# Transposing q on VectorE in 32x32 blocks, in a linear-attention and feed-forward kernel

## The chip, the cores and the metric

One core of a Trainium2 chip runs the whole program. The metric is device microseconds of one execution. The engines are TensorE (PE, with its weight loads as PEld), VectorE (DVE), ScalarE (ACT), GpSimd (POOL) and SyncE (SP), which issues all the DMAs here.

## The reference

Linear attention over 8 batches, 8 heads, 576 tokens and 64 places of d, then a feed-forward block over all 4608 tokens:

```python
q_s = softmax(q, over d)            # exp(q - max), divided by (sum + 1e-9)
k_s = softmax(k, over the tokens)
kv  = einsum('bhsd,bhse->bhde', k_s, v)
x   = einsum('bhsd,bhde->bhse', q_s, kv)     # then (tokens, 512)
h   = x @ w_in                                # 512 -> 2048
g   = h where h >= 1; 0 where h <= -1; (h + 1)**2 / 4 between
out = g @ w_out                               # 2048 -> 512
```

## The kernel before

Tokens are handled in 9 chunks of 512. For each chunk there are 16 units of feed-forward, one for each 128 columns of the 2048. A unit written 3.5 below is unit 5 of chunk 3. A unit's first half (`s1`, L679) is 12 matmuls of 128x512 into a PSUM tile `h`; then ACT does relu and square (`g_relu`, `g_square`), DVE the minimum (`g_min`, L698), ACT the high half (`g_hi`, `gh`), DVE the low half (`g_lo`, `gl`, L706); its second half (`s2`, L717) is 12 matmuls into four PSUM tiles `o`, which are copied to SBUF (`osb`) and stored at the end of a chunk. Each fp32 product is done as three fp32r matmuls of high and low parts. PE does s1 of the next unit before s2 of this one, so the chain of relu to g_lo runs beside PE's work. `h` has two buffers, `r` (the relu's output) three.

While chunk c is in the feed-forward, the attention of chunk c+1 is prepared in four parts, one for each pair of heads (0 to 3). A tile name such as `q_4_1` is chunk 4, pair 1. For a pair:

- k: loaded, maximum over the tokens (`k_max`, tile `m2`, DVE; then `partition_all_reduce` on POOL), subtracted on DVE (`k_sub`), exponential on ACT, and multiplied with v on PE (`kv_mm`, 20 small matmuls into `kv`). Its reciprocal sums (`kv_z`), high part (`kv_hi`, ACT) and low part (`kv_lo`, DVE) follow. Chunks 0 and 1 handle k in another way, and chunk 8 has no k.
- q: loaded as 128 token rows by 4 x 128, maximum over each 64 places on DVE (`q_max`), subtracted on POOL (`q_rows`), exponential on ACT (`q_exp`), summed on DVE (`q_sum`, with the added constant and the reciprocal), multiplied on POOL (`q_rows`), transposed on PE with four 128x128 matmuls against an identity (`q_tr`, tile `tp` in PSUM), then split into a high part (`q_hi`, ACT) and a low part (`q_lo`, DVE).
- `x_mm` on PE multiplies the two with kv; `x_hi` and `x_lo` split the result for s1 of the next chunk.

The order of instructions on every engine is written out by a planner (`Plan`): each operation is given an engine, an estimated time, a due time and what it depends on, and buffers are represented by rings. The planner's list is then emitted as it is, so each engine works through its queue in order, and an instruction that waits holds up all that stands behind it on its engine. The small tiles of the pool `sm` (maxima and sums) have no ring in the plan; the tile framework adds the waits that their buffers need. `port=True` tells the planner to keep an operation apart from others on the port that DVE and POOL share. In chunks from 2 on, `q_tr` and `kv_mm` are one operation of the plan.

Of the kernel before, what the change touches and what calls it, by code (L numbers as in the profile page):

```python
# [11 lines left out]
F32 = mybir.dt.float32  # L12
# [16 lines left out]
NF = DF // P  # L29


NLOAD, NST, NR = 2, 4, 3

KT = 2

WARM = 9

# [39 lines left out]
class Plan:  # L77
# [103 lines left out]
def tile_linear_attention_then_ffn(  # L181
# [18 lines left out]
    nc = tc.nc  # L200
    NB = k.shape[0] + KT
    NT = out.shape[0]
# [8 lines left out]
    wk = ctx.enter_context(tc.tile_pool(name="wk", bufs=1))  # L211
# [3 lines left out]
    sm = ctx.enter_context(tc.tile_pool(name="sm", bufs=4))  # L215
# [23 lines left out]
    def ring(tag, n):  # L239
        return rings.setdefault(tag, Ring(n))  # L240
# [86 lines left out]
    xs, xdone, kvdone, kvread, kfs = {}, {}, {}, {}, []  # L327

    def attention(c, pr, due, step, slack):


        n = f"{c}_{pr}"
        first = c == 0
        after = 0.0 if first else START
        has_k = c < NB
        t = {}

        def at(stage):
# [46 lines left out]
        rpk, rpq = room(f"ps {ktag}", 1), room(f"ps {qtag}", 1)  # L385
# [51 lines left out]
        def kv_mm():  # L437
            t["kv"] = kpool.tile([P, D + 1], F32, tag=ktag, name=f"kv_{n}")
            for j in range(KJ):
                r = slice(0, SR if c < KT and j == KJ - 1 else P)  # L440
                for i in range(2):
                    d = slice(i * D, (i + 1) * D)
                    nc.tensor.matmul(  # L443
                        t["kv"][d, :],
                        t["k"][r, j, d],
                        t["v"][r, j, i * (D + 1) : (i + 1) * (D + 1)],
                        start=(j == 0),
                        stop=(j == KJ - 1),
                        tile_position=(0, i * D),
                    )  # L450
# [30 lines left out]
        def kv_lo():  # L481
# [4 lines left out]
            for i in range(2):  # L486
# [7 lines left out]
                    ALU.subtract,  # L494
                )

        def q_max():
            t["qf"] = t["q"].rearrange("p j (h d) -> p (j h) d", h=2)
            t["qm"] = sm.tile([P, 2 * NJ], F32, tag="qm", name=f"qm_{n}")
            nc.vector.tensor_reduce(t["qm"], t["qf"], AX.X, ALU.max)  # L500

        def q_rows(what, alu):
            def emit():
                rows = t[what].unsqueeze(2).broadcast_to([P, 2 * NJ, D])
                nc.gpsimd.tensor_tensor(t["qf"], t["qf"], rows, alu)  # L505

            return emit

# [1 line left out]
            nc.scalar.activation(t["q"], t["q"], AF.Exp)  # L510

        def q_sum():
            z = sm.tile([P, 2 * NJ], F32, tag="qz", name=f"qz_{n}")
            nc.vector.tensor_reduce(z, t["qf"], AX.X, ALU.add)
            nc.vector.tensor_scalar(z, z, EPS, None, ALU.add)
            t["qrz"] = sm.tile([P, 2 * NJ], F32, tag="qrz", name=f"qrz_{n}")
            nc.vector.reciprocal(t["qrz"], z)  # L517

        def q_tr():
            t["tp"] = qpool.tile([P, NJ, P], F32, tag=qtag, name=f"tp_{n}")  # L520
            for j in range(NJ):
                nc.tensor.transpose(t["tp"][:, j, :], t["q"][:, j, :], ident)  # L522
# [43 lines left out]
        kvready = []  # L566
        if has_k:
            if c < KT:
                et = room("ps h", 2) if first else rpq
                km = do("DVE", 0.75, 0, kt_max, lk)  # L570
                ke = do("ACT", 0.9, 1, kt_exp, km)
                kz = do("DVE", 0.32, 4, kv_z, ke)
                tr = do("PE", 0.75, 2, kt_tr, ke, *rpk.wait(), *et.wait())
# [5 lines left out]
                kc = do("ACT", 0.58, 2.5, kt_copy, tr, *rk.wait(), other=copies[0])  # L579
# [22 lines left out]
        if first or not has_k:  # L602
            tr = do("PE", 0.6, 3.6, q_tr, qn, *rpq.wait())
        else:

            def q_tr_kv_mm():
                q_tr()
                kv_mm()

            deps = [qn, ke, lv, *rpq.wait()] + ([kc] if c < KT else rpk.wait())  # L610
            tr = mm = do("PE", 1.3, 3.6, q_tr_kv_mm, *deps)
            if c >= KT:
                rpk.take(mm)
                kz = do("DVE", 0.32, 4, kv_z, mm)
            rk.free(mm)
        rpq.take(tr)
        rq.free(tr)
        if has_k:
            rv.free(mm)
            if first:  # L620
# [3 lines left out]
                kvready = [kf]  # L624
# [8 lines left out]
            else:  # L633
# [3 lines left out]
                kvready = [kl]  # L637
                rpk.free(kl)
        if first:
            qh = do(  # L640
                "ACT", 0.59, 4.1, q_32, tr, *rqh.wait(), other=[("DVE", 0.69, False)]
            )
            rqh.take(qh)
            xm = do("PE", 1.05, 4.5, x_mm32, qh, *kvready)
            early_users.append(xm)
            rqh.free(xm)
        else:
            rql = room("wk ql", 1)
# [4 lines left out]
            xm = do("PE", 0.8, 4.6, x_mm, ql, *kvready, kvdone.get((c - 1, pr)))  # L653
            rqh.free(xm)
            rql.free(xm)
            kvread[c - 1, pr] = xm
# [126 lines left out]
    for pr in range(NPAIR):  # L783
        attention(0, pr, 2.0 * pr, 1.5, 0.0)
# [90 lines left out]
```

## Time and profile before

| | |
|---|---|
| median of three runs | 891.9 us (891.73 to 892.34) |
| the profiled execution | 894.39 us, span 892.6 us |
| PE busy | 878.3 us, 98% |
| DVE busy | 429.2 us, 48% |
| ACT busy | 416.9 us, 47% |
| POOL busy | 140.1 us, 16% |

PE is the busy engine. Matmuls are pipelined, so the duration in a PE row is longer than the distance to the next start; what a matmul takes of PE's time is read from the starts. POOL's busy time leaves out what it spends between its own instructions around `partition_all_reduce`, where its idle time is put down to "issue".

### The profile page before, as it was taken

How to read it: one execution, taken by the hardware profiler on the slowest of the kernel's cores; microseconds unless marked ns; L12 is line 12 of the kernel's file. 1: busy time of each engine (PE TensorE's matmuls, PEld its weight loads, DVE VectorE, ACT ScalarE, POOL GpSimd, SP SyncE). 2: the span in 40 equal slices, each digit the busy share in tenths (PEclk: the TensorE clock that was granted, in tenths of full speed). 3: DMA queues.
4: the chain of work that ended last, by engine and by line, in shares of the span. 5: the costliest groups of instructions: out<-in, count | busy, mean ns of one | idle time of the engine just before them, and what ended most of it. 6: DMA issues, size and time to landing. Idle time of an engine off the chain costs nothing.

```text
span 892.6 us, 11623 instructions
## 1 busy us (share of the span) xinstructions
PE 878.3 (98%) x4486; PEld 722.8 (81%) x4486; DVE 429.2 (48%) x817; ACT 416.9 (47%) x736; POOL 140.1 (16%) x136
## 2 busy tenths in 40 slices
PE   7899999999999999999999999999999999999997
PEld 6588887888888888888888888888888888888886
DVE  6989865444544444454444444445434333323221
ACT  6787754443444444344434544444443444433333
POOL 5554521111111101111011110111011000000000
PEclk8999999999999999999999999999999999999999
DMA  8466512111211120020111121112100000000001
GB/s 320 163 218 208 194 68 78 42 42 42 89 42 42 42 81 27 28 79 24 66 42 42 43 89 42 42 42 89 42 14 12 36 24 12 1 17 32 1 1 47
DMA packets 24247, 57.27 MB, mean 64 GB/s; under 512 B 2688, under 2 KB 2688, under 8 KB 24192
## 3 DMA queue, kind: packets, MB, share of 16 engines
q1 hardware_dynamic: 24192, 56.54, 19.0%
q8 instruction: 35, 0.57, 0.3%
q14 instruction: 20, 0.16, 0.1%
HBM read 47.09 MB, written 9.44 MB: 63 GB/s over the span
## 4 chain that ended last, share of the span: by engine, by line
PE 95%; DVE 2%; DMA 1%; issue 1%; ACT 1%; POOL 0%; SPq 0%; DVEq 0%; ACTq 0%; POOLq 0%
PE o L717 44%; PE h L679 43%; PE x L546 3%; PE kv L443 3%; PE tp L522 2%; DMA q<-in_q 1%; DVE st L291 0%; PE x L538 0%; DVE st L288 0%; PE ep L414 0%; DMA k<-in_kt 0%; POOL q L505 0%; DMA out<-osb 0%; DVE qm L500 0%; ACT osb L225 0%
## 5 line engine op out<-in xcount | busy, mean ns | idle before, releaser
L692 ACT ACTIVATE r<-h,half 128x512 f32<-128x512 f32 x144 | 99.2, 689 | 356.6 <-PE h L679 356.5
L698 DVE SCALAR_TENSOR_TENSOR h<-h,r 128x512 f32<-128x512 f32 x144 | 100.6, 699 | 313.9 <-ACT r L695 313.6
L717 PE MATMUL o<-wl,gh 128*128 128x512 f32 x576 | 228.6, 397 | 1.8 <-ACT gh L702 1.1
L679 PE MATMUL h<-xl,wh 128*128 128x512 f32 x576 | 226.2, 393 | 0.4 <-DVE xl L561 0.4
L717 PE MATMUL o<-wh,gl 128*128 128x512 f32 x576 | 225.5, 391 | 0.9 <-DVE gl L706 0.9
L679 PE MATMUL h<-xh,wl 128*128 128x512 f32 x576 | 224.6, 390 | 0.9 <-POOL wl L302 0.9
L717 PE MATMUL o<-wh,gh 128*128 128x512 f32 x576 | 224.9, 390 | 0.0
L679 PE MATMUL h<-xh,wh 128*128 128x512 f32 x576 | 224.3, 389 | 0.0
L706 DVE TENSOR_TENSOR gl<-h,gh 128x512 fp32r<-128x512 f32 x144 | 99.0, 687 | 73.4 <-ACT gh L702 73.1
L717 PEld LDWEIGHTS o<-wl,gh 128*128 128x128 f32 x576 | 108.4, 188 | 25.5 <-ACT gh L702 2.0
L717 PEld LDWEIGHTS o<-wh,gl 128*128 128x128 f32 x576 | 108.4, 188 | 25.3 <-DVE gl L706 2.2
L679 PEld LDWEIGHTS h<-xh,wl 128*128 128x128 f32 x576 | 108.1, 188 | 24.3 <-POOL wl L302 1.8
L679 PEld LDWEIGHTS h<-xl,wh 128*128 128x128 f32 x576 | 108.3, 188 | 23.5 <-DVE xl L561 0.8
L679 PEld LDWEIGHTS h<-xh,wh 128*128 128x128 f32 x576 | 108.3, 188 | 22.1 <-issue 0.2
L717 PEld LDWEIGHTS o<-wh,gh 128*128 128x128 f32 x576 | 108.5, 188 | 21.2
L702 ACT CAST gh<-h 128x512 fp32r<-128x512 f32 x144 | 84.2, 585 | 74.4 <-DVE h L698 74.1
L695 ACT ACTIVATE r<-r 128x512 f32<-128x512 f32 x144 | 91.1, 633 | 4.3
L505 POOL TENSOR_TENSOR q<-q,qm 128x512 f32<-128x512 f32 x36 | 39.2, 1091 | 224.1 <-issue 107.9
L505 POOL TENSOR_TENSOR q<-q,qrz 128x512 f32<-128x512 f32 x36 | 38.0, 1055 | 158.6 <-DVE qrz L517 111.9
L302 POOL TENSOR_TENSOR wl<-st,wh 128x512 fp32r<-128x512 f32 x32 | 43.0, 1360 | 46.4 <-ACT wh L298 45.1
L426 POOL PARTITION_ALL_REDUCE m<-m x24 | 17.4, 725 | 178.9 <-DVE m L393 118.9
L291 DVE SCALAR_TENSOR_TENSOR st<-st 128x512 uint32<-128x512 uint32 x32 | 29.3, 917 | 2.6 <-ACT st L285 0.2
(72 smaller groups left out, 595.1 us busy)
## 6 DMA issues: line engine op xcount, KB each, us to landing
st<-in_w SPq DMA_DIRECT2D x32, 512.0 KB, 4.5
v<-in_v SPq DMA_DIRECT2D x32, 325.0 KB, 4.3
q<-in_q SPq DMA_DIRECT2D x36, 256.0 KB, 3.4
out<-osb SPq DMA_DIRECT2D x36, 256.0 KB, 2.0
k<-in_k SPq DMA_DIRECT2D x24, 320.0 KB, 3.2
kt<-in_kt SPq DMA_DIRECT2D x4, 288.0 KB, 4.9
k<-in_kt SPq DMA_DIRECT2D x4, 288.0 KB, 3.2
```

The lines of the kernel that those rows point to most:

```text
L291: nc.vector.scalar_tensor_tensor(t["lw"], t["hw"], 3, t["lw"], ALU.logical_shift_left, ALU.bitwise_or)
L302: nc.gpsimd.tensor_tensor(lo, t["lw"].bitcast(F32), f32(hi), ALU.subtract)
L443: nc.tensor.matmul(t["kv"][d, :], t["k"][r, j, d], t["v"][r, j, i * (D + 1) : (i + 1) * (D + 1)], start=(j == 0), stop=(j == KJ - 1), tile ...
L505: nc.gpsimd.tensor_tensor(t["qf"], t["qf"], rows, alu)
L546: nc.tensor.matmul(t["x"][:, :, p0:p1], lhs, rhs[:, :, p0:p1], start=(i == 0), stop=(i == 2),)
L679: nc.tensor.matmul(t["h"], lhs[:, r], rhs, start=(cc == 0 and i == 0), stop=(cc == NPAIR - 1 and i == 2),)
L692: nc.scalar.activation(t["r"], t["h"], AF.Relu, bias=half[:, :1], scale=0.5)
L695: nc.scalar.activation(t["r"], t["r"], AF.Square)
L698: nc.vector.scalar_tensor_tensor(t["h"], t["h"], 1.0, t["r"], ALU.max, ALU.min)
L702: nc.scalar.copy(t["gh"], t["h"])
L706: nc.vector.tensor_tensor(t["gl"], t["h"], f32(t["gh"]), ALU.subtract)
L717: nc.tensor.matmul(outs[c, j], lhs[:, s], rhs, start=(f == 0 and i == 0), stop=(f == NF - 1 and i == 2),)
```

## The change

In chunks 2 to 8, q is laid out in memory so that a partition holds one of 32 tokens with one of four blocks of 32 places of d (two heads times two halves of d), and along the row lie 16 blocks of 32 places, each of another group of tokens. VectorE's transpose of 32x32 blocks then gives the tile that four transposes on PE gave, in SBUF instead of PSUM. A token's 64 places now lie in two quadrants of 32 partitions. So `q_max` and `q_sum` reduce over 32 places each, and `q_both` joins the two halves: four copies of 32x16 swap neighbouring quadrants, and one 128x16 operation takes the maximum or the sum of the two. The joined maximum (`qm`) has one buffer, the joined sum (`qrz`) two; before, they had four. `r` gets two buffers instead of three. `kv_mm` is an operation of its own on PE, without q. The buffer of `x` in PSUM is taken at `x_mm` instead of at the transpose. Chunks 0 and 1 stay as they were.

```diff
-NLOAD, NST, NR = 2, 4, 3
+NLOAD, NST, NR = 2, 4, 2
...
+QT, QB = 2, 32
+NQ = P // QB
...
+        rows = c < QT
+        nrow = 2 * NJ if rows else T // QB
+
+        def q_both(part, alu, tag):
+            if rows:
+                return part
+            other = sm.tile([P, nrow], F32, tag="qo", name=f"{tag}o_{n}", bufs=1)
+            both = sm.tile(
+                [P, nrow], F32, tag=tag, name=f"{tag}_{n}", bufs=1 + (tag == "qrz")
+            )
+            for i in range(NQ):
+                r, o = (slice(x * QB, (x + 1) * QB) for x in (i, i ^ 1))
+                nc.vector.tensor_copy(other[r], part[o])
+            nc.vector.tensor_tensor(both, part, other, alu)
+            return both
+
         def q_max():
...
-            nc.vector.tensor_reduce(t["qm"], t["qf"], AX.X, ALU.max)
+            qm = sm.tile([P, nrow], F32, tag="qz", name=f"qm_{n}", bufs=2)
+            nc.vector.tensor_reduce(qm, t["qf"], AX.X, ALU.max)
+            t["qm"] = q_both(qm, ALU.max, "qm")
...
             nc.vector.tensor_reduce(z, t["qf"], AX.X, ALU.add)
+            z = q_both(z, ALU.add, "qrz")
             nc.vector.tensor_scalar(z, z, EPS, None, ALU.add)
...
+        def q_blocks():
+            t["tp"] = wk.tile([P, NJ, P], F32, tag="qt", name=f"tp_{n}")
+            nc.vector.transpose(
+                t["tp"].rearrange("p j d -> p (j d)"), t["q"].rearrange("p j d -> p (j d)")
+            )
...
-        qm = do("DVE", 0.68, 0.5, q_max, lq)
+        qm = do("DVE", 0.68 if rows else 1.4, 0.5, q_max, lq)
...
-        qz = do("DVE", 1.13, 2.2, q_sum, qe)
+        qz = do("DVE", 1.13 if rows else 1.85, 2.2, q_sum, qe)
...
-            tr = mm = do("PE", 1.3, 3.6, q_tr_kv_mm, *deps)
...
+            rqt = room("wk qt", 1)
+            tr = do("DVE", 0.65, 3.6, q_blocks, qn, *rqt.wait(), port=True)
+            rqt.take(tr)
+            if has_k:
+                mm = do("PE", 0.95, 3.6, kv_mm, ke, lv, *rpk.wait())
...
-            ql = do("DVE", 0.69, 4.2, q_lo, qh, *rql.wait())
+            ql = do("DVE", 0.69, 4.2, q_lo, qh, *rql.wait(), port=not rows)
...
+    qb = qq[QT:].reshape(-1, NQ, QB, NJ, NPAIR, 2, D // QB, QB)
+    qb = qb.transpose(0, 4, 5, 6, 2, 3, 1, 7).reshape(-1, NPAIR, P, 2 * NJ * D)
```

The planner sets a new order from it. Three places show what moves. In the rows below, a line number, an operation, out<-in and a shape stand in a row, "x3" is a count, and the brackets name the engines and DMA queues that the instruction waits for.

PE, at unit 3.5, before: behind the last matmuls of s1 come the transposes of `q_4_1` and the kv product of the same pair, then s2 of unit 3.4.

```order
L679 MATMUL h_3_5_3301<-xl_3_3_2996,wh5_0_111 128x512
L679 MATMUL h_3_5_3301<-xh_3_3_2985,wh5_0_111 128x512
L679 MATMUL h_3_5_3301<-xh_3_3_2985,wl5_0_112 128x512
L522 MATMUL tp_4_1_3322<-ident_90,q_4_1_2904 128x128 [waits DMAHW4_49,PE_49,Pool_49]
L522 MATMUL tp_4_1_3322<-ident_90,q_4_1_2904 128x128 x3
L443 MATMUL kv_4_1_3327<-v_4_1_2910,k_4_1_2900 64x65 [waits DMAHW5_49,DMAHW3_49]
L443 MATMUL kv_4_1_3327<-v_4_1_2910,k_4_1_2900 64x65 x9
L717 MATMUL o_3_0_3143<-wl4_1_110,gh_3_4_3299 128x512 [waits Activation_49]
```

The same place on PE in the changed kernel:

```order
L728 MATMUL h_3_5_3457<-xl_3_3_3144,wh5_0_111 128x512
L728 MATMUL h_3_5_3457<-xh_3_3_3129,wh5_0_111 128x512
L728 MATMUL h_3_5_3457<-xh_3_3_3129,wl5_0_112 128x512
L447 MATMUL kv_4_1_3484<-v_4_1_3044,k_4_1_3042 64x65 [waits DMAHW6_49,DMAHW5_49,PE_49]
L447 MATMUL kv_4_1_3484<-v_4_1_3044,k_4_1_3042 64x65 x9
L766 MATMUL o_3_0_3298<-wl4_1_110,gh_3_4_3461 128x512 [waits Activation_49]
```

The kv product stands where it stood, without the transposes and without the wait for POOL.

DVE, at the start of chunk 1, before: from g_lo of unit 0.15 to g_lo of unit 1.0.

```order
L706 TENSOR_TENSOR gl_0_15_1468<-h_0_15_1415,gh_0_15_1462 128x512 [waits Activation_49]
L227 COPY osb_0_1_1495<-o_0_1_513 128x512 [waits PE_49]
L698 SCALAR_TENSOR_TENSOR h_1_0_1464<-h_1_0_1464,r_1_0_1482 128x512 [waits DVE_49,Activation_49]
L430 TENSOR_TENSOR k_2_0_1294<-k_2_0_1294,m2_2_0_1383 128x640 [waits Pool_49]
L706 TENSOR_TENSOR gl_1_0_1513<-h_1_0_1464,gh_1_0_1507 128x512 [waits Activation_49]
```

The same stretch of DVE in the changed kernel (`qmo` is the copy with swapped quadrants, and the last `qm` the joined maximum):

```order
L755 TENSOR_TENSOR gl_0_15_1494<-h_0_15_1428,gh_0_15_1488 128x512 [waits Activation_49]
L571 TENSOR_TENSOR ql_2_0_1499<-tp_2_0_1447,qh_2_0_1482 128x512
L526 TENSOR_REDUCE qm_2_2_1504<-q_2_2_1461 128x16 [waits DMAHW6_49]
L516 COPY qmo_2_2_1506<-qm_2_2_1504 32x16 [waits DVE_49]
L516 COPY qmo_2_2_1506<-qm_2_2_1504 32x16 x3
L517 TENSOR_TENSOR qm_2_2_1507<-qm_2_2_1504,qmo_2_2_1506 128x16 [waits DVE_49,Pool_49]
L231 COPY osb_0_1_1532<-o_0_1_513 128x512 [waits PE_49]
L747 SCALAR_TENSOR_TENSOR h_1_0_1490<-h_1_0_1490,r_1_0_1519 128x512 [waits Activation_49]
L434 TENSOR_TENSOR k_2_0_1295<-k_2_0_1295,m2_2_0_1399 128x640
L755 TENSOR_TENSOR gl_1_0_1551<-h_1_0_1490,gh_1_0_1545 128x512 [waits Activation_49]
```

The low part of `q_2_0` and the maximum of `q_2_2`, with its join, have come ahead of `osb_0_1`, g_min and g_lo of unit 1.0, and the join's last operation waits for POOL.

POOL at the same time, before (`ISA` rows are the steps around `partition_all_reduce`):

```order
L302 TENSOR_TENSOR wl15_1_1147<-st15_1_1299,wh15_1_1146 128x512 [waits DMAHW2_49,Activation_49]
L426 ISA
L426 ISA m2_2_0_1383<-m2_2_0_1383 128x128 [waits DVE_49]
L505 ISA
L505 TENSOR_TENSOR q_2_1_1373<-q_2_1_1373,qm_2_1_1434 128x512 [waits DMAHW4_49,DVE_49,PE_49]
```

POOL in the changed kernel:

```order
L306 TENSOR_TENSOR wl15_1_1147<-st15_1_1303,wh15_1_1146 128x512 [waits DMAHW2_49,Activation_49]
L430 ISA
L430 ISA m2_2_0_1399<-m2_2_0_1399 128x128 [waits DVE_49]
L532 ISA
L532 TENSOR_TENSOR q_2_1_1386<-q_2_1_1386,qm_2_1_1455 128x512 [waits DMAHW4_49,DVE_49,PE_49]
L532 TENSOR_TENSOR q_2_2_1461<-q_2_2_1461,qm_2_2_1507 128x512 [waits DMAHW6_49,DVE_49]
```

Up to the subtraction for `q_2_1` POOL's queue is the same; the one for `q_2_2` has moved directly behind it.

More of the change, by code (lines that the diff above doesn't have):

```diff
@@ L512, in q_sum @@
         def q_sum():
-            z = sm.tile([P, 2 * NJ], F32, tag="qz", name=f"qz_{n}")
+            z = sm.tile([P, nrow], F32, tag="qz", name=f"qz_{n}", bufs=2)
             nc.vector.tensor_reduce(z, t["qf"], AX.X, ALU.add)
+            z = q_both(z, ALU.add, "qrz")
             nc.vector.tensor_scalar(z, z, EPS, None, ALU.add)
-            t["qrz"] = sm.tile([P, 2 * NJ], F32, tag="qrz", name=f"qrz_{n}")
+            if rows:
+                t["qrz"] = sm.tile([P, nrow], F32, tag="qrz", name=f"qrz_{n}", bufs=2)
+            else:
+                t["qrz"] = z
             nc.vector.reciprocal(t["qrz"], z)
+        def q_blocks():
[3 more added lines that the diff above has]
+            )
         def q_tr():
@@ L596, in attention @@
             parts = [kvread.get((c - 2, pr))]
-        qm = do("DVE", 0.68, 0.5, q_max, lq)
+        qm = do("DVE", 0.68 if rows else 1.4, 0.5, q_max, lq)
         qs = do("POOL", 1.1, 1, q_rows("qm", ALU.subtract), qm, port=True)
         qe = do("ACT", 0.63, 2, q_exp, qs)
-        qz = do("DVE", 1.13, 2.2, q_sum, qe)
+        qz = do("DVE", 1.13 if rows else 1.85, 2.2, q_sum, qe)
         qn = do("POOL", 1.1, 3, q_rows("qrz", ALU.mult), qz, port=True)
-        if first or not has_k:
+        if first:
             tr = do("PE", 0.6, 3.6, q_tr, qn, *rpq.wait())
-        else:
+        elif rows:
             def q_tr_kv_mm():
@@ L608, in q_tr_kv_mm @@
                 kv_mm()
-            deps = [qn, ke, lv, *rpq.wait()] + ([kc] if c < KT else rpk.wait())
-            tr = mm = do("PE", 1.3, 3.6, q_tr_kv_mm, *deps)
-            if c >= KT:
+            tr = mm = do("PE", 1.3, 3.6, q_tr_kv_mm, qn, ke, kc, lv, *rpq.wait())
+            rk.free(mm)
+        else:
+            rqt = room("wk qt", 1)
[3 more added lines that the diff above has]
+                mm = do("PE", 0.95, 3.6, kv_mm, ke, lv, *rpk.wait())
                 rpk.take(mm)
                 kz = do("DVE", 0.32, 4, kv_z, mm)
-            rk.free(mm)
-        rpq.take(tr)
+                rk.free(mm)
+        if rows:
+            rpq.take(tr)
         rq.free(tr)
@@ L650, in attention @@
             rqh.take(qh)
-            ql = do("DVE", 0.69, 4.2, q_lo, qh, *rql.wait())
+            ql = do("DVE", 0.69, 4.2, q_lo, qh, *rql.wait(), port=not rows)
             rql.take(ql)
-            xm = do("PE", 0.8, 4.6, x_mm, ql, *kvready, kvdone.get((c - 1, pr)))
+            xw = [ql, *kvready, kvdone.get((c - 1, pr))]
+            if not rows:
+                rqt.free(ql)
+                xw += rpq.wait()
+            xm = do("PE", 0.8, 4.6, x_mm, *xw)
+            if not rows:
+                rpq.take(xm)
             rqh.free(xm)
```

15 lines of the change are left out of this document (9 added, 6 removed).

## The prediction

> **What bounds the kernel now.** I read the busy line and the chain first, then a table of windows, then the groups, then single rows. The busy line gives PE 98% of the span, and the chain of waits runs over PE for 95% of it. The window from 300 to 400 us, steady state, has PE busy for all of it at granted clock 1.00, with DVE and ACT under half. So what leaves PE there shortens the run, and what is added to DVE costs nothing until a result comes late. The fourth row is the work that leaves: 144 transposes, of which chunks 0 and 1 keep 32.
>
> ```profile
> PE 878.3 (98%) x4486; PEld 722.8 (81%) x4486; DVE 429.2 (48%) x817; ACT 416.9 (47%) x736; POOL 140.1 (16%) x136
> ...
> PE 95%; DVE 2%; DMA 1%; issue 1%; ACT 1%; POOL 0%; SPq 0%; DVEq 0%; ACTq 0%; POOLq 0%
> ...
> 300.00:400.00 100.00, 100.00 (x543) 82.89 (x542) 46.79 (x98) 45.82 (x82) 11.94 (x13) 1.00 0.17 54
> ...
> L522 PE MATMUL tp<-ident,q 128*128 128x128 f32 x144 | 22.3, 278 | 0.6 <-POOL q L505 0.6
> ```
>
> **What PE loses.** Matmuls overlap, so the cost is a distance between starts. The first rows are a pair with a kv product, the last three a pair of chunk 8, which has none (columns: start, duration).
>
> ```profile
> 395.58 0.60 PE L522 MATMUL tp<-ident,q 128*128 128x128 f32 x4
> 396.11 0.80 PE L443 MATMUL kv<-v,k 128*64 128x65 f32 x20
> 396.84 0.50 PE L717 MATMUL o<-wl,gh 128*128 128x512 f32 x1
> 397.18 0.39 PE L717 MATMUL o<-wh,gh 128*128 128x512 f32 x1
> 397.41 0.39 PE L717 MATMUL o<-wh,gl 128*128 128x512 f32 x1
> ...
> 777.00 0.60 PE L522 MATMUL tp<-ident,q 128*128 128x128 f32 x4
> 777.35 0.48 PE L717 MATMUL o<-wl,gh 128*128 128x512 f32 x1
> 777.67 0.40 PE L717 MATMUL o<-wh,gh 128*128 128x512 f32 x1
> ```
>
> From the transposes' start to the kv product's is 396.11 - 395.58 = 0.53 us. In chunk 8, from 777.00 to the second matmul behind is 0.67 us; one 512-wide matmul takes 397.41 - 397.18 = 0.23, so 0.44 is the transposes'. The kv product stays where it was, and is bounded at its own 0.73 plus the same tail as before, since a matmul still stands on both sides of it. Saving: 24 pairs x 0.53 + 4 x 0.44 = 14.5 us. Ends: 28 x 0.35 (777.35 - 777.00, if the tail stays with what follows) = 9.8, and 28 x 0.60 (the row's duration) = 16.8. I take 14.5, from the distances of starts.
>
> **What DVE, ACT and POOL gain.** Rows: the maximum, the low half, a pair of quadrant-sized operations, the high half, a copy from SBUF, the landing of a q load (its last figure), and one sum as it stands in time.
>
> ```profile
> L500 DVE TENSOR_REDUCE qm<-q 128x8 f32<-128x512 f32 x36 | 24.3, 678 | 1.8 <-DMA q<-in_q 1.7
> L534 DVE TENSOR_TENSOR ql<-tp,qh 128x512 fp32r<-128x512 f32 x32 | 21.8, 680 | 0.0
> L530 ACT CAST qh<-tp 128x512 fp32r<-128x512 f32 x32 | 18.6, 583 | 0.3 <-PE tp L522 0.3
> L298 ACT CAST wh<-st 128x512 fp32r<-128x512 f32 x32 | 20.0, 655 | 3.5 <-DVE st L291 3.5
> L488 DVE SCALAR_TENSOR_TENSOR kvt<-kv,rz,kvt 64x64 fp32r<-64x64 f32 x56 | 15.6, 279 | 0.4
> ...
> q<-in_q SPq DMA_DIRECT2D x36, 256.0 KB, 3.4
> ...
> 398.04 0.67 DVE L514 TENSOR_REDUCE qz<-q 128x8 f32<-128x512 f32 x1
> 398.74 0.17 DVE L515 TENSOR_SCALAR qz<-qz 128x8 f32<-128x8 f32 x1
> 398.95 0.20 DVE L517 RECIPROCAL qrz<-qz 128x8 f32<-128x8 f32 x1
> 399.07 0.64 DVE L706 TENSOR_TENSOR gl<-h,gh 128x512 fp32r<-128x512 f32 x1
> ```
>
> A join is four copies of 32x16 and one 128x16 operation. No row has the copy; between 0.17 (128x8) and 0.28 (64x64 across partitions) I take 0.20, nearest in elements, so a join is 1.0 us, ends 0.8 and 1.4. A pair pays two joins, 2.0 us. The 32x32 transpose of 128x512 has no row either; a one-input pass over 512 elements takes 0.68, and four such passes 2.7; I take 0.68 and keep 2.7 as the upper end. Per pair DVE gains 2.7 us (up to 5.5), over 28 pairs 75 us (up to 154) on top of 429: under two thirds of the span. The high half now reads SBUF: 0.583 to 0.655, 2 us of idle ACT in all. The reductions, POOL's two passes and the q load keep their elements and bytes. On SP the q loads move ahead, pair 2 of chunk 2 past chunk 0's four stores; it waits only for the transpose of pair 0 a unit earlier and lands 3.4 us after its issue (median), and the stores follow the copies of unit 1.0, so nothing queues behind it. The third buffer of r costs nothing: a unit's relu waits for its h tile, h has two buffers, and h is freed by g_lo, which stands behind the g_min that frees r.
>
> What hides DVE's gain is the distance between a unit's g_lo and the matmul that reads it, since PE does another half unit first:
>
> ```profile
> 393.08 0.69 DVE L706 TENSOR_TENSOR gl<-h,gh 128x512 fp32r<-128x512 f32 x1 [0.65 <-ACT gh L702]
> ...
> 404.01 0.70 DVE L698 SCALAR_TENSOR_TENSOR h<-h,r 128x512 f32<-128x512 f32 x1 [1.51 <-ACT r L695]
> ...
> 411.54 0.69 DVE L706 TENSOR_TENSOR gl<-h,gh 128x512 fp32r<-128x512 f32 x1 [0.65 <-ACT gh L702]
> ...
> 414.50 0.39 PE L717 MATMUL o<-wh,gl 128*128 128x512 f32 x1
> ```
>
> g_lo ends at 393.77 and is read at 397.41, 3.6 us of cover; the one that ends at 412.23 is read at 414.50, 2.3 us. From the end of g_lo at 399.71 to the next g_min at 404.01 DVE has 4.3 us more. The fullest stretch of the new order there (one sum with join 2.1, kv_lo 0.57, k_max 1.0) takes 3.7. It fits, the more so as the transposes read what POOL finished some five units earlier, so in steady state the DVE work costs nothing. If a join took 1.4, it would still fit.
>
> **The wait that is added.** At the start of chunk 1 the order puts the join of pair 2's maximum (chunk 2) ahead of copy osb_0_1, g_min and g_lo of unit 1.0. Its result has one buffer, which POOL's subtraction for pair 1 still reads, so the DVE queue stands until that ends. The planner's rings don't hold this buffer. In the trace of before that subtraction is late, behind partition_all_reduce:
>
> ```profile
> 128.14 0.72 POOL L426 PARTITION_ALL_REDUCE m<-m  x1 [5.56 <-DVE h L698]
> 135.79 1.04 POOL L505 TENSOR_TENSOR q<-q,qm 128x512 f32<-128x512 f32 x1 [6.93 <-issue]
> ...
> 134.41 0.69 DVE L706 TENSOR_TENSOR gl<-h,gh 128x512 fp32r<-128x512 f32 x1
> 135.80 1.19 DVE L393 TENSOR_TENSOR m<-m,k 128x128 f32<-128x128 f32 x1
> ...
> L393 DVE TENSOR_TENSOR m<-m,k 128x128 f32<-128x128 f32 x24 | 7.9, 330 | 0.8
> ...
> 133.79 0.59 ACT L702 CAST gh<-h 128x512 fp32r<-128x512 f32 x1 [0.89 <-DVE h L698]
> 138.60 0.57 ACT L225 COPY osb<-o 128x512 f32<-128x512 f32 x1
> ...
> 136.34 0.39 PE L717 MATMUL o<-wl,gh 128*128 128x512 f32 x1
> 139.22 0.50 PE L717 MATMUL o<-wl,gh 128*128 128x512 f32 x1 [0.62 <-ACT osb L225]
> ```
>
> Everything that feeds POOL there is unchanged, so the subtraction again ends at 136.83. Then on DVE: the join's last operation to 137.0, osb_0_1 to 137.7, g_min to 138.4; on ACT the cast gh to 139.05. PE's first o matmul of unit 1.0 starts at 139.05 instead of 136.34: 2.7 us late. Behind it ACT does two exponentials, osb_0_2, a relu and osb_0_3 (0.5 to 0.6 each between starts), done at 141.9; the matmul that had waited until 139.22 waits until then, again 2.7. In unit 1.1 DVE does k_max (1.0) and two sums with joins (4.2) from 139.75 on, so g_min comes at 145.0 and g_lo ends near 147; PE, behind s1 of unit 1.2 and a kv product, wants it at 146.7: 0.2 more (nothing with a 0.8 us join, 1.0 with 1.4). The term is 2.9 us, ends 2.7 and 3.7. A second such wait, at unit 1.6, I put at nothing: what it stands on is due a unit earlier, and 2.3 us of cover is behind it.
>
> **The clock.** An early stretch shows what a pause can cost (timeline rows, then windows; the third figure from the end is the granted clock):
>
> ```profile
> 34.31 0.51 PE L717 MATMUL o<-wl,gh 128*128 128x512 f32 x1 [1.09 <-ACT gh L702]
> 35.95 0.50 PE L717 MATMUL o<-wh,gl 128*128 128x512 f32 x1 [0.91 <-DVE gl L706]
> 39.24 0.63 PE L717 MATMUL o<-wh,gl 128*128 128x512 f32 x1
> ...
> 37.00:38.00 1.00, 1.00 (x4) 0.71 (x4) 1.00 (x2) 0.97 (x3) 0.41 (x1) 0.50 0.59 229
> 40.00:41.00 1.00, 1.00 (x5) 0.79 (x5) 0.93 (x3) 1.00 (x3) 1.00 (x2) 0.88 0.19 78
> ```
>
> Two waits, 2.0 us together, are followed by clock 0.50, which is over early in the window from 40 us. At half clock for some 3.2 us a matmul takes 0.43 instead of 0.23 from start to start, so PE loses 1.5, of which about 0.3 falls into the wait for osb_0_3: a drop behind the new 2.7 us pause would add 1.2. Whether it comes can't be read from one instance; I leave it out of the sum and make it a rival.
>
> The Trainium skill, "TensorE: Matmul & The Clock Gate", in "Why this matters for your kernels", advises no idle gap above about 3 us between bursts, since one idle window returns the array to half rate. By that advice 2.7 us would pass and the sum stands without the 1.2. The rows above show half rate after less, so the trace agrees with the half rate and not with the length.
>
> **The sum.** 14.5 - 2.9 = 11.6 us. The profiled execution took 894.39 (span 892.6), so 882.8 by it; it lies 2.5 above the median of the runs, 891.9, from which I get **880.3**.
>
> **Rivals.**
> - The wait, and the clock drops behind it: 881.5. For it: two pauses of 2.0 us in all did it at 37 us; against: a pause must lie badly.
> - No wait that PE sees, because POOL's subtraction comes earlier or the order's wait is satisfied by then: 891.9 - 14.5 = 877.4. Against: the same POOL rows stand ahead of it in both orders.
> - Steady units come late too: DVE waits for POOL or for q loads twice a pair, and PE loses 0.1 to 0.3 us in each of 28 pairs, 3 to 8 us: 883 to 889. For it: POOL needs 7 us to return from each partition_all_reduce (128.86 to 135.79); against: the cover of 2.3 us.
> - Slower than before: the joins in the stretch between g_lo and g_min eat the cover in every pair. It decides at 11.6 / 28 = 0.41 us a pair, so the stretch must take 4.3 + 2.3 + 0.4 = 7.0 us; 2.6 of it is known (1.1 + 0.57 + 1.0), so each of five small operations must take 0.87, four times the nearest row. A port collision with POOL can do that to one (1.19 for the row at 135.80, where POOL's pass starts at 135.79, against a mean of 0.33), not to all: 892.5 to 896.
> - The transposes go but PE gains only the lower end, 9.8: 885.0; inside the range.
>
> **Chances.** My forecast 0.42, clock drop 0.22, no wait 0.15, late units 0.14 (and the lower end within it), slower 0.04, same 0.03. The range 877 to 886 holds the first three and half of the fourth. A measurement of this kernel tells about 0.2% (1.8 us) from no change. Faster is 0.93.
>
> **What would show it.** 112 fewer PE rows of tp; PE's 100 us windows still full after 200 us, with a unit with kv 0.5 shorter. At chunk 1's start, a DVE wait of some 6 us for POOL ahead of osb_0_1 and a PE wait near 2.7 for gh. DVE busy 480 to 510 us. Wrong would be: new PE waits on gl or gh in chunks 2 to 7, a 32x32 transpose far above 0.7, or a PE distance around the lone kv product that keeps the transposes' 0.5.

## The result, and the profile after

The changed kernel takes 883.4 us (median of four runs, 881.52 to 884.61) against 891.8 for the kernel before beside it: a ratio of 0.9904, 95% interval 0.9885 to 0.9923. It is 8.4 us faster. The forecast was 880.3, range 877 to 886: the direction and the mechanism held, and the size of the gain was 3 us too large. On a second chip the same kernel took 883.19 against 893.42 (0.9892, 0.987 to 0.9915), a gain of 10.2. Of all executions reported below one stands apart, the profiled one of the last kernel: it took 2220.96 us where the other four took 879, so that kernel's ratio goes by the four and no trace of it is shown; the cause is open.

The profiled execution of the changed kernel is the slowest of the four, 884.61. The page's busy line and the chain of waits, and the groups of the new operations (busy us, mean ns, idle time ahead):

```profile
PE 866.0 (98%) x4374; PEld 709.1 (80%) x4374; DVE 499.4 (57%) x1117; ACT 424.6 (48%) x744; POOL 142.5 (16%) x136
...
PE 95%; DVE 2%; DMA 1%; issue 1%; ACT 0%; SPq 0%; POOL 0%; DVEq 0%; ACTq 0%
...
L516 DVE COPY qmo<-qm 32x16 f32<-32x16 f32 x112 | 20.3, 182 | 2.1
L552 DVE STREAM_TRANSPOSE tp<-q 128x512 f32<-128x512 f32 x28 | 19.9, 709 | 3.0 <-POOL q L532 2.2
L517 DVE TENSOR_TENSOR qm<-qm,qmo 128x16 f32<-128x16 f32 x28 | 4.9, 175 | 8.3 <-POOL q L532 7.4
L567 ACT CAST qh<-tp 128x512 fp32r<-128x512 f32 x32 | 19.9, 623 | 0.3 <-PE tp L559 0.3
```

One window of it (busy time of PE, PEld, DVE, ACT and POOL, then the granted clock), and the first two of PE's waits (us in total, times, longest):

```profile
200.00:800.00 600.00, 600.00 (x3028) 494.88 (x3027) 323.36 (x761) 268.54 (x464) 64.54 (x65) 1.00 0.13 44
```

```profile
PE o L766 <- ACT gh L751: 4.3, 3, 3.0
PE kv L447 <- DMA v<-in_v: 2.2, 1, 2.2
```

PE has 112 matmuls fewer and is full for all of 200 to 800 us at clock 1.00, so nothing that DVE gained (70 us) is late there. PE has two new waits that are not part of the start-up, both for `gh`: 3.04 us at unit 1.0 and 0.19 at unit 1.1. The long one stands where it was forecast. From the timelines of POOL, DVE, ACT and PE there (start, duration; in brackets the idle time ahead and what ended it):

```profile
127.34 0.72 POOL L430 PARTITION_ALL_REDUCE m<-m  x1 [5.61 <-DVE h L747]
135.59 1.04 POOL L532 TENSOR_TENSOR q<-q,qm 128x512 f32<-128x512 f32 x1 [7.53 <-issue]
...
129.49 0.71 DVE L516 COPY qmo<-qm 32x16 f32<-32x16 f32 x4
136.66 0.17 DVE L517 TENSOR_TENSOR qm<-qm,qmo 128x16 f32<-128x16 f32 x1 [6.46 <-POOL q L532]
136.76 0.68 DVE L231 COPY osb<-o 128x512 f32<-128x512 f32 x1
137.36 0.69 DVE L747 SCALAR_TENSOR_TENSOR h<-h,r 128x512 f32<-128x512 f32 x1
...
138.08 0.58 ACT L751 CAST gh<-h 128x512 fp32r<-128x512 f32 x1 [6.01 <-DVE h L747]
...
138.72 0.50 PE L766 MATMUL o<-wl,gh 128*128 128x512 f32 x1 [3.04 <-ACT gh L751]
```

DVE has done the four copies by 130.2 and then stands 6.46 us, until POOL's subtraction releases the single buffer of the joined maximum. POOL is back from `partition_all_reduce` only at 135.59, 7.53 us after it. `osb_0_1`, g_min, `gh` and PE's first o matmul follow one behind the other. Comparing the two traces by the first matmul of each unit, the changed kernel is 0.83 us ahead at unit 1.0 (a start-up difference) and 2.15 behind at unit 1.4, so it lost 2.98 us net. The kv product of `q_2_0`'s pair stands in that stretch too, without its transposes, and what that saved (0.43, see below) is already taken off. The waits themselves cost 3.4 us: 2.92 up to unit 1.2 and 0.49 behind it, for the 0.19 and for the o matmuls after it, some of which start 0.34 to 0.39 us apart instead of 0.23.

From then on it gains 0.43 us a pair, evenly: 0.85 behind at unit 2.0 and 7.82 ahead at unit 7.0, 8.67 over 20 pairs. Chunk 8's four pairs gain 1.94, or 0.485 each. So 24 x 0.434 + 4 x 0.485 = 12.4 us are saved, where 14.5 were forecast, and 12.4 - 3.4 = 9.0 lies between the two chips' 8.4 and 10.2. (From unit 1.0 to the last unit the two traces differ by 8.9.) The missing 2 us show at the kv product at unit 3.12 (pair 3 of chunk 4), the place that the prediction read (timeline of PE in the changed kernel):

```profile
393.17 0.39 PE L728 MATMUL h<-xh,wl 128*128 128x512 f32 x1
393.49 0.80 PE L447 MATMUL kv<-v,k 128*64 128x65 f32 x20
394.22 0.50 PE L766 MATMUL o<-wl,gh 128*128 128x512 f32 x1
394.55 0.39 PE L766 MATMUL o<-wh,gh 128*128 128x512 f32 x1
```

The kv product still takes 0.73 from its start to the next (393.49 to 394.22) and the same 0.33 behind it. But it now starts 0.32 us after the last 512-wide matmul, where one 512-wide matmul follows another in 0.23. Before, the transposes stood there and started 0.23 behind that matmul. The step of 0.09 in front of kv is not new, though. The prediction read the four transposes from one merged row; singly they start at 395.58, 395.69, 395.80 and 395.91. A narrow window of the kernel before shows the last of them and the first two matmuls of kv:

```profile
395.91 0.27 PE L522 MATMUL tp<-ident,q 128*128 128x128 f32 x1
396.11 0.28 PE L443 MATMUL kv<-v,k 128*64 128x65 f32 x2
```

One transpose follows another in 0.11, and kv follows the last in 0.20. So the same 0.09 stood in front of kv before the change: of the 0.53, 4 x 0.11 = 0.44 was the transposes', and the rest stayed. What goes with it in both kernels is kv's first weight load (PEld), here in the changed one:

```profile
393.48 0.61 PEld L447 LDWEIGHTS kv<-v,k 128*64 128x64 f32 x18 [0.35 <-issue]
```

It starts together with kv's first matmul (393.49; before, both at 396.11), where the load for the 512-wide matmul at 393.17 starts at 392.94, beside the matmul ahead of it. Why kv's does not is open.

### The profile page after: what moved, and what is told of

The parts are those of the page before. It is cut to its first block, busy times and chain, and to the rows that moved or that the text cites. A ratio compares the mean times of both kernels' runs of the same rounds, so it can differ in the third digit from the quotient of the medians.

```text
span 882.8 us, 11653 instructions
## 1 busy us (share of the span) xinstructions
PE 866.0 (98%) x4374; PEld 709.1 (80%) x4374; DVE 499.4 (57%) x1117; ACT 424.6 (48%) x744; POOL 142.5 (16%) x136
## 4 chain that ended last, share of the span: by engine, by line
PE 95%; DVE 2%; DMA 1%; issue 1%; ACT 0%; SPq 0%; POOL 0%; DVEq 0%; ACTq 0%
PE o L766 45%; PE h L728 43%; PE x L583 3%; PE kv L447 3%; DMA v<-in_v 1%; DVE st L295 0%; PE ep L418 0%; PE tp L559 0%; PE x L575 0%; DVE st L292 0%; DVE h L747 0%; DMA out<-osb 0%; DVE xl L598 0%; SPq L368 0%; DVE qrzo L516 0%
## 5 line engine op out<-in xcount | busy, mean ns | idle before, releaser
L532 POOL TENSOR_TENSOR q<-q,qm 128x512 f32<-128x512 f32 x36 | 41.7, 1159 | 187.3 <-DVE qm L517 132.3
L447 PEld LDWEIGHTS kv<-v,k 128*64 128x64 f32 (+1 forms) x640 | 22.9, 142 | 13.0 <-issue 9.5
```

The costliest lines, as they stand in the source:

```text
L447: nc.tensor.matmul(t["kv"][d, :], t["k"][r, j, d], t["v"][r, j, i * (D + 1) : (i + 1) * (D + 1)], start=(j == 0), stop=(j == KJ - 1), tile ...
L532: nc.gpsimd.tensor_tensor(t["qf"], t["qf"], at, alu)
```

## Experiments

Theory: the gain is PE's distance of starts, less a step that stays in front of kv, less the waits at chunk 1; DVE's additions are hidden. Rivals: the small third term, that steady units come late; that the third buffer of `r` matters; that the clock takes the rest.

### One of four transposes left

The kernel before, with only the first of the four transposes in the 24 pairs of chunks 2 to 7:

```diff
-            for j in range(NJ):
+            for j in range(NTR if KT <= c < NB else NJ):     # NTR = 1
...
+            if KT <= c < NB and NTR < NJ:
+                t["tp"] = t["tp"][:, :1, :].broadcast_to([P, NJ, P])
```

> The kernel before with one transpose in place of four in the 24 pairs of chunks 2 to 7; the high and low halves read that one 128x128 block four times over, so three quarters of the transposed q are left out. Same order. Theory A (a short matmul behind a 512-wide one pays some 0.1 us once, whichever it is, and each further transpose costs 0.13): the distance of starts from the first transpose to the second o matmul behind the kv product falls from 1.60 us by 0.40, nearly all of the 0.435 that removing all four brought. Theory B (each transpose costs a quarter of 0.435, no fixed part): it falls by 0.33. Over 24 pairs 9.6 or 7.8 us.

It took 887.44 us against 893.87 beside it (one execution each). From unit 2.0 to 7.0 it gains 6.07 us on the kernel before, 0.304 a pair, for three transposes. First this kernel, then the kernel before at the same place:

```profile
392.36 0.39 PE L682 MATMUL h<-xh,wl 128*128 128x512 f32 x1
392.59 0.27 PE L523 MATMUL tp<-ident,q 128*128 128x128 f32 x1
392.79 0.80 PE L444 MATMUL kv<-v,k 128*64 128x65 f32 x20
393.53 0.50 PE L720 MATMUL o<-wl,gh 128*128 128x512 f32 x1
```

```profile
395.35 0.40 PE L679 MATMUL h<-xh,wl 128*128 128x512 f32 x1
```

Four transposes hold kv back by 0.53, one by 0.20 (392.59 to 392.79): three are worth 0.33, or 0.11 each, which is what theory B expected, a quarter each and no fixed part. (The matmuls behind kv stand a little further apart in this kernel, 0.03 in all, which leaves the 0.304.) The single transpose starts 0.23 behind the 512-wide matmul, as one 512-wide matmul behind another does, and kv 0.20 behind it: the 0.09 again stands in front of kv. With the last transpose gone, kv follows the 512-wide matmul at 0.23 + 0.09 = 0.32. So the four together were worth 4 x 0.11 = 0.44 here, not 0.53; the changed kernel gains 0.434.

### Twice and six times the join, four times the transpose

Three kernels put more work on DVE, at places that leave PE and the order of the rest alone: the copies of each join done twice or six times, or each 32x32 transpose done four times (into the same tile).

```diff
-            for i in range(NQ):
+            for i in [*range(NQ)] * 2:      # and * 6
```

```diff
-            nc.vector.transpose(
+            for _ in range(4):
+                nc.vector.transpose(
```

> The changed kernel with the four copies of each join done twice (0.71 us more for each of 56 joins, 40 us of DVE). Same order. If the cover between g_lo and the matmul that reads it holds, PE loses nothing in chunks 2 to 7, and only unit 1.1, where two sums stand ahead of g_min and gh was already 0.19 late, loses 1.4 us. Rival (DVE on the path): about 40 us more.

> The changed kernel with the 32x32 transpose done four times (0.6 us more each time, 1.8 for each of 28 pairs, 50 us of DVE): the upper end of its price in the prediction. The stretch with xl, ql and the transpose then takes 0.6 + 0.6 + 2.5 = 3.7 us, within the 4.3. Nothing in steady state; at unit 1.3, where the transpose had waited for POOL until 152.74, up to 1 us.

> The changed kernel with the four copies of each join done six times (3.55 us more for each join, 199 us of DVE; DVE near 80% busy). The fullest stretch between g_lo and g_min then takes 3.7 + 3.55 = 7.3 us, against 4.3 us of distance and 2.3 to 3.6 of cover (6.6 to 7.9). By my cover arithmetic PE loses 0 to 0.7 us in a pair, 0 to 20 us over the run, and some 6.5 more at unit 1.1. If DVE's time is paid in full: some 200 us more.

Against 893.87 for the kernel before beside them they took 888.3, 888.45 and 989.44 us (one execution each; 888.45 is the transposes'). In the first two, each chunk from 2 to 7 gains on the kernel before what the changed kernel gains, 1.72 to 1.73 us, so 0.7 us more for each join, or 2.1 more for each transpose (711 ns each), is hidden there. What they lose is lost between units 1.0 and 1.8: 5.4 us with joins done twice, 4.9 with four transposes, against 2.5 in the changed kernel. Each of the two also has 3.4 us at half clock in there, which is part of it. PE's waits, of the joins first:

```profile
PE o L766 <- ACT gh L751: 5.8, 3, 2.8
```

```profile
PE o L767 <- ACT gh L752: 3.8, 2, 2.8
PE o L767 <- DVE gl L756: 2.5, 2, 1.6
```

So the cover of 2.3 and 3.6 us is there in steady state, and is used up in chunk 1 only: at unit 1.0 and behind it, at units 1.1 (joins) and 1.4 (transposes).

With the join done six times my cover arithmetic failed outright; the loss was 106 us and not the few tens that I had allowed. Its waits of PE, three stretches of its timelines (DVE, then twice PE), and its windows:

```profile
PE o L766 <- ACT gh L751: 40.6, 15, 8.1
PE x L583 <- DVE kvt L492: 17.6, 11, 2.1
PE o L766 <- DVE gl L755: 14.4, 9, 3.0
```

```profile
433.37 4.71 DVE L516 COPY qrzo<-qz 32x16 f32<-32x16 f32 x24
438.70 0.67 DVE L747 SCALAR_TENSOR_TENSOR h<-h,r 128x512 f32<-128x512 f32 x1
439.28 0.57 DVE L492 SCALAR_TENSOR_TENSOR kvt<-kv,rz,kvt 64x64 fp32r<-64x64 f32 x2
...
439.90 0.39 PE L583 MATMUL x<-qh,kvt 128*128 128x256 f32 x1 [2.07 <-DVE kvt L492]
...
548.94 0.36 PE L583 MATMUL x<-qh,kvt 128*128 128x192 f32 x1 [2.01 <-DVE kvt L492]
```

```profile
550.00:551.00 1.00, 1.00 (x4) 0.80 (x4) 0.93 (x4) 0.87 (x2) 0.00 (x0) 0.76 0.00 0
551.00:552.00 1.00, 1.00 (x4) 0.71 (x3) 0.35 (x2) 0.62 (x2) 0.00 (x0) 0.50 0.00 0
...
200.00:800.00 600.00, 554.50 (x2714) 443.85 (x2714) 455.17 (x1668) 237.15 (x417) 65.66 (x67) 0.96 0.13 42
```

I had counted only g_lo, which PE reads half a unit later. Behind the sum's join in DVE's queue also stands kv_lo, whose result (`kvt`) the x product wants without that cover: ten waits of 1.45 to 2.07 us in chunks 2 to 7. It isn't all: most chunks also have one wait of about 3.5 us for `gh` and one of 1.5 for `gl`, where the arithmetic had allowed 0.7 a pair at most. And a wait costs more than its length: behind the 2.01 us at 548.94 the granted clock is at 0.50 from about 550.5 on. From 200 to 800 us PE stands 45.5 us, 17.6 of it for `kvt`, and runs at a mean clock of 0.96. Against the changed kernel 39 us are lost from the start to unit 2.0, with the longest wait (8.1), and 67 behind it.

### The third buffer of r

```diff
-NLOAD, NST, NR = 2, 4, 3
+NLOAD, NST, NR = 2, 4, 2
```

> The kernel before with two buffers for r instead of three, nothing else. My theory: no difference (under 0.2%), since a unit's relu already waits for its h tile, freed behind the g_min that frees r. Rival: the third buffer covered some of DVE's late minima in chunk 0, where DVE is 90% busy; then 1 to 3 us slower, with PE waits for gh in chunk 0.

The kernel before with two buffers of r: 893.74 us, ratio 1.0004 (0.999 to 1.0019). It costs nothing that shows, as the prediction said.

### The changed kernel once more: the clock

> The changed kernel once more, for the comparison on the same chip. By its trace PE lost 3.0 us at unit 1.0 and gained 0.435 us in each of 24 pairs and 0.485 in each of 4: 9.4 us less than before. The runs told 8.4 with a spread of 3 us, and the mean granted clock went with the time (0.998 at 881.5, 0.995 at 883.4). If PE's pause of 3.0 us lets the clock fall in some executions and not in others, times come in two groups 1.5 to 2 us apart, the slower one with the lower clock, and the kernel with four buffers comes in fewer slow ones. If the spread comes from the start (loads), it is the same in both.

883.19 us. Its profiled execution (883.85 us) shows the rival that was priced at 1.2 us. The first o matmul of unit 1.0 and two that follow soon after, then windows of 1 us (the clock is the third figure from the end):

```profile
136.13 0.79 PE L766 MATMUL o<-wl,gh 128*128 128x512 f32 x1 [2.86 <-ACT gh L751]
...
138.00 0.63 PE L766 MATMUL o<-wh,gh 128*128 128x512 f32 x1
138.42 0.63 PE L766 MATMUL o<-wh,gl 128*128 128x512 f32 x1
```

```profile
134.00:135.00 1.00, 0.00 (x0) 0.00 (x0) 0.93 (x3) 0.00 (x0) 0.71 (x2) 1.00 0.00 0
135.00:136.00 1.00, 0.00 (x0) 0.00 (x0) 1.00 (x2) 0.51 (x2) 0.38 (x1) 0.76 0.28 109
136.00:137.00 1.00, 0.87 (x2) 0.65 (x3) 1.00 (x3) 1.00 (x3) 0.00 (x0) 0.50 0.40 154
141.00:142.00 1.00, 1.00 (x4) 0.81 (x3) 0.90 (x5) 0.00 (x0) 0.38 (x1) 0.50 0.08 16
142.00:143.00 1.00, 1.00 (x5) 0.77 (x4) 0.41 (x1) 0.56 (x1) 0.35 (x1) 0.83 0.03 8
```

The wait is as long as in the first profile (2.86 and 3.04 us), but here the clock is halved from about 135.5 to 142.3, and matmuls start 0.42 apart instead of 0.23. Units 1.0 to 1.8 cost 4.2 us instead of 2.5, so the drop is worth about 1.6. In the first profile the clock stays at 1.00 behind the longer wait. So the same program has both; which it gets isn't decided by the length of that one wait. The Trainium skill, "TensorE: Matmul & The Clock Gate", "Why this matters for your kernels", advises no idle gap above about 3 us: the drops here came behind 2.86 and 2.01, and none behind 3.04, so no run here shows such a length as the dividing line.

What goes with the drops in these traces is how a wait lies against the steps of the clock. The granted clock changes only at steps of 3.41 us: here it is halved for two of them, in the kernel with six joins for one (550.5 to 553.9). Take all 13 traces of kernels that ran 880 to 990 us, from 20 us to the last matmul, at full clock. PE stood 1.9 us or more within one step 21 times, and the next step was at half clock each time; with less than 1.6 us within a step it never was; with 1.6 to 1.9 it was in six cases of eight. The 2.86 us put 2.2 into one step. The 3.04 us were split by the end of a step at 137.5 into 1.8 and 1.2. This is read from the traces; no run moved a wait to test it.

### More buffers for the joined maximum

If the wait at unit 1.0 comes from one buffer, more buffers should give back what it costs, or part of it where ACT would be late anyway. First four buffers; then four buffers and a planner's price for `k_all` that is nearer to what POOL needs, so that the order leaves POOL time.

```diff
-                [P, nrow], F32, tag=tag, name=f"{tag}_{n}", bufs=1 + (tag == "qrz")
+                [P, nrow], F32, tag=tag, name=f"{tag}_{n}", bufs=4 - 2 * (tag == "qrz")
...
-                mb = do("POOL", 8.6, 0.1, k_all, km, made[NF - 1, 1])
+                mb = do("POOL", 14.0, 0.1, k_all, km, made[NF - 1, 1])   # second kernel only
```

> The changed kernel with four buffers for the joined maximum instead of one; the order on every engine is the same, and DVE's wait for POOL ahead of osb_0_1 at the start of chunk 1 is gone. Theory A (the single buffer opens the gap, but ACT would be late anyway, since it stands at two exponentials that need POOL's subtractions ahead of osb_0_2, the relu of unit 1.1 and osb_0_3): POOL's second subtraction ends at 137.7 by the trace of the changed kernel, so ACT gets to osb_0_2 at 138.2 and is done with osb_0_3 near 139.9; the last o matmuls of unit 1.0 start there instead of at 141.3. Gain 1.4 us of the 3.0. PE waits for osb_0_2, not for gh. Theory B (the buffer is all of it): 3.0 us less than the changed kernel. Theory C (POOL's lateness alone): no gain.

> Four buffers for the joined maximum, and the plan is told 14.0 us for partition_all_reduce instead of 8.6 (about what POOL needs from the pass before it to the pass behind it: 122 to 136 us in the trace). That moves ACT's two exponentials and k's behind the copies osb of chunk 0. If the rest of the 3.0 us is ACT standing at POOL, PE's wait at unit 1.0 goes below 0.7 us and the time falls by 2.5 to 3.0 us against the changed kernel, to about 880.5. If the new order brings other waits, they show as PE waits for gh, gl or x in chunks 1 to 7, and the gain is smaller.

Four buffers took 886.9 us, ratio 0.9931 (0.9911 to 0.9951), slower than the changed kernel's 883.19 beside it, which no theory had. The second took 882.86 (0.9894, 0.9874 to 0.9913). The wait itself went much as theory A says: none for `gh` is left at unit 1.0 (the 1.1 below is the start-up's), and one of 1.0 for `osb` comes in its place. PE's waits with four buffers:

```profile
PE o L766 <- ACT gh L751: 1.3, 2, 1.1
PE o L766 <- ACT osb L229: 1.0, 1, 1.0
```

Between units 1.0 and 1.8 this kernel loses 0.7 us on the kernel before, against 2.5 in the changed kernel; the 1.8 between lie above theory A's 1.4 and below theory B's 3.0. But each later chunk gains only 1.24 us instead of 1.73, and the difference lies in units 13 to 15 and 0 of each chunk, where PE does not wait. Its o matmuls in units 13 to 15 start 0.233 us apart on average, in the changed kernel 0.227, with the same order of instructions. Units 2 to 11 of a chunk take what they take in the changed kernel. The units that differ read the weights that are allocated last, behind the pool of small tiles that had grown by 192 bytes per partition.

### Only the address

To test this without touching any wait: the changed kernel with 64, or 128, unused bytes per partition at the front of that pool.

```diff
+    for i in range(1):      # and range(2)
+        sm.tile([P, 16], F32, tag=f"pad{i}", name=f"pad{i}", bufs=1)
```

> The changed kernel with one unused tile of 64 bytes per partition at the front of the pool of small tiles: every instruction and wait stands as before, but all tiles allocated behind that pool (kvf and the weights wh, wl of rows 12 to 15) lie 64 bytes higher, at 64 and no longer at 0 modulo 128, as with four buffers of the joined maxima (192 bytes). Theory A, the address costs: the o matmuls of units 13 to 15 start 0.233 us apart as there, where the changed kernel has 0.227; a chunk loses 0.45 to 0.5 us; 8 chunks make 3.6 to 4.0, so 886.8 to 887.2 against 883.2. Theory B, the extra buffers cost it by what waits on them: nothing here waits otherwise, so 0.227 and 882.5 to 884.

> The changed kernel with 128 unused bytes per partition at the same place: the late weights lie at 0 modulo 128 and at 128 modulo 256. Theory A1, what costs is a start off 128 bytes: o start distances 0.227 in units 13 to 15, 882.5 to 884. Theory A2, what costs is a start off 256 bytes: 0.233 as with 64 bytes, 886.5 to 887.5. Theory B, no address matters: as A1 here, but then the run with 64 bytes shows nothing either.

They took 888.75 us (0.9955, 0.994 to 0.9969) and 886.7 (0.9938, 0.9919 to 0.9958; before 893.4 beside both). PE's wait for `gh` at unit 1.0 is there, 2.2 and 3.1 us long. Matmuls of s1 in unit 2.14, the first and the last of an unbroken stretch, in the changed kernel, then with 64 bytes, and the latter's window:

```profile
309.37 0.39 PE L728 MATMUL h<-xl,wh 128*128 128x512 f32 x1
...
311.87 0.39 PE L728 MATMUL h<-xh,wl 128*128 128x512 f32 x1
```

```profile
309.80 0.39 PE L730 MATMUL h<-xl,wh 128*128 128x512 f32 x1
...
311.90 0.40 PE L730 MATMUL h<-xl,wh 128*128 128x512 f32 x1
```

```profile
300.00:312.00 12.00, 12.00 (x72) 9.97 (x73) 8.53 (x23) 6.57 (x12) 1.80 (x2) 1.00 0.17 55
```

Eleven starts in 2.50 us, 0.227 each, against nine in 2.10, 0.233 each, at granted clock 1.00 and with PE full. Over chunks 2 to 7 the means in units 12 to 15 are, in us:

| | h | o in 13 to 15 |
|---|---|---|
| changed kernel | 0.227 | 0.227 |
| 64 bytes more | 0.233 | 0.231 |
| 128 bytes more | 0.233 | 0.233 |
| 192 bytes more (four buffers) | 0.230 | 0.233 |

So the address costs, and it is not the buffers; how it does is open. (The small tiles themselves move by the same bytes, but PE reads none of them.) It is about 0.57 us a chunk with 64 bytes (from unit 2.0 to 4.0 it gains 1.16 a chunk on the kernel before, the changed kernel 1.73), 5 us over nine chunks; between 888.75 and the changed kernel's 883.19 (before 893.42 there) lie 5.6. With 128 bytes the distances give as much, and the times a loss of 3.5. Theory A1, by which 128 bytes would be harmless, fell: of the four places only the first is free. A full 256 bytes more was not tried.

### Both mended

Two buffers for the joined maximum (64 bytes more), and three instead of four each for `z` and `rz` (64 bytes less), so that the late weights lie where the changed kernel has them; then the same with the price of `k_all`.

```diff
+            t["rz"] = sm.tile([P, 1], F32, tag="rz", name=f"rz_{n}", bufs=3)
...
+                [P, nrow], F32, tag=tag, name=f"{tag}_{n}", bufs=2
...
+                mb = do("POOL", 14.0, 0.1, k_all, km, made[NF - 1, 1])   # second kernel only
```

> The joined maxima get two buffers (64 bytes more), and z and rz three each for four (64 bytes less), so that the late weights lie where the changed kernel has them; the order of instructions is that of the changed kernel. Address theory with the wait as forecast: no wait of PE for gh over 0.5 us at unit 1.0, o distances 0.227 in units 13 to 15, a chunk 1.7 us shorter than before in chunks 2 to 7: 883.2 less 2 to 3 gives 880.2 to 881.2. Rival, more buffers cost by themselves: 886 to 887 as with four. Rival, two buffers are not enough and the wait stays: 883 to 884.

> The same two and three buffers, and k_all planned at 14.0 us for 8.6, so that the planner starts nothing on POOL's heels at chunk 1's start. With four buffers and the late weights at 64 modulo 128 this was 882.9 on the chip, with 1.8 us gained between units 1.0 and 1.8. Address theory: the same without 3.6 to 4.0 of the start distances: 878.9 to 879.3. Rival, more buffers cost by themselves: 882.5 to 883.5.

They took 881.33 us (0.9878, 0.9858 to 0.9897) and 879.33 (0.985, 0.9832 to 0.9868), before 893.4 beside both. In the first, the distances in units 13 to 15 are 0.227 again, each chunk gains 1.73, and the only wait for `gh`, 1.1, is the start-up's (at 32.3 us); the one for `osb` is at unit 1.0:

```profile
PE o L766 <- ACT osb L229: 1.2, 1, 1.2
PE o L766 <- ACT gh L751: 1.1, 1, 1.1
```

It loses 0.7 us between units 1.0 and 1.8 instead of 2.5. The second has the lowest median of all that ran, and its interval lies below both of the changed kernel's (0.9885 to 0.9923, 0.987 to 0.9915). With four buffers the same price had given 882.86; of the 3.5 us between, the address theory had forecast 3.6 to 4.0.

## Why the prediction was right, and where it was off

- **What PE gains: right in kind, mis-sized.** 24 x 0.53 should have been 24 x 0.434 (10.4 us), and 4 x 0.44 measured 4 x 0.485 (1.9): 12.4 instead of 14.5. The step that was off is the reading of 396.11 - 395.58 as the transposes' own: it held 0.09 us that stands in front of kv and stays when they go. "The kv product stays where it was, and is bounded at its own 0.73 plus the same tail as before" has the tail right (0.33) and leaves out what stands ahead. A distance around the lone kv product had been listed as a sign of being wrong, and not priced; the trace of before had it, in the single starts that the merged row hides.
- **The added waits: right in mechanism, somewhat small.** 2.9 forecast, 3.4 measured, within the ends of 2.7 and 3.7. At unit 1.0 it was 2.92 for 2.7 (DVE stood 6.46 us for POOL where 6 were forecast, PE 3.04 for `gh`), and at unit 1.1 0.49 for 0.2. The queue order, the single buffer and POOL's late return were enough to find it. Two buffers take the wait for `gh` away, though one of 1.2 for `osb` is left, and 881.33 results, 1.9 less than the changed kernel's 883.19 (before 893.4 beside each).
- **The cover: right for the change, wrong beyond it.** The join was priced at 1.0 us and takes 0.9 (0.71 for four copies and 0.17), the transpose at 0.68 and takes 0.709; DVE ends at 499.4 (480 to 510 forecast) and is hidden from 200 to 800 us. The rival of late steady units, 0.1 to 0.3 us a pair, is refuted by the full windows. But the arithmetic behind it, cover of g_lo alone, doesn't hold further out: with the join done six times it missed the reader of `kvt` and was too small for `gh` and `gl`.
- **The clock: happens, in some executions.** Not behind this wait in the first profile, about 1.6 us in the second, against 1.2 priced. That the first profile came without it was luck: its wait lay across the end of a clock step. How much of the scatter from 881.5 to 885.7 the drops make is not shown.
- **The third buffer of r:** nothing that shows, as forecast.

With 12.4 for 14.5 and 3.4 for 2.9 the same sum gives 891.9 - 9.0 = 882.9; the rest to 883.4 is within the scatter of the start-up, where the first matmul of the feed-forward starts anywhere between 22.2 and 25.1 us in these profiles. That the two misses point the same way is why the gain came out 3 us too large.

## What to carry to other kernels

When work is taken out between two neighbours on a pipelined engine, price it from single starts, not from a merged row, and ask which part of the distance belongs to the neighbour and will stay. Look for single buffers that an in-order queue takes early: the wait lands on whatever stands behind. And when a harmless edit of small tiles moves the time by 0.5%, compare the distances of the matmuls by unit before explaining it by waits: here the address of tiles allocated later had moved.

## What the runs showed of the hardware

- The place of a weight tile in SBUF changes the rate of fp32r matmuls that read it: 0.227 us from start to start became 0.230 to 0.233 with the tiles 64, 128 or 192 bytes higher, whether the weights are the stationary side (h) or the moving one (o).
- A run of 128-wide transposes on PE starts 0.23 us behind a 512-wide matmul and costs 0.11 each. The kv product (20 small matmuls of 128x65) starts about 0.09 later than a regular neighbour would, 0.20 behind a transpose and 0.32 behind a 512-wide matmul, and its first weight load starts only with it. The x products, 128 to 512 wide, follow a 512-wide matmul at 0.227 and show no such step.
- Two waits of PE of nearly the same length, 2.86 and 3.04 us in two executions of one program, halved the clock for 6.8 us in the first and left it at 1.00 in the second. The clock changes at steps of 3.41 us, and in these traces 1.9 us or more of standing within one step always halved the next, while less than 1.6 never did.
